# Linear attention and a two-layer network in one kernel: keys and values with the token halves on the partition halves

## The chip, the cores and the metric

The kernel runs on one core of one Trainium2 chip. The metric is device time in microseconds (us); shorter is better. The kernel before takes 294.94 us, the median of 8 runs (294.67 to 295.29).

A core's engines, as the profile names them: PE (TensorE, matmuls; PEld is its weight load), DVE (VectorE), ACT (ScalarE), POOL (GpSimd, which here issues the loads) and SP (SyncE, which issues stores and small transfers).

## The reference

```python
def _attn_ref(q, k, v):                      # each [8 batches, 8 heads, 576 tokens, 64]
    phi = lambda x: np.where(x > 0, x, np.exp(x) - 1.0) + 1.0
    q_p, k_p = phi(q), phi(k)
    kv = np.einsum('bhsd,bhse->bhde', k_p, v)
    z = np.sum(k_p, axis=2)
    num = np.einsum('bhsd,bhde->bhse', q_p, kv)
    den = np.einsum('bhsd,bhd->bhs', q_p, z)[..., None] + 1e-06
    return num / den

def _moe_ref(x, w_in, w_out):                # x: [4608, 512], the heads side by side
    h = x @ w_in                             # w_in [512, 2048]
    return (h - np.tanh(h)) @ w_out          # w_out [2048, 512]
```

Inputs and output are float32; the kernel computes matmuls in bfloat16 with float32 sums.

## The kernel before, in words

**The dense part.** The 4608 tokens are taken in nine chunks `c` of 512. For a chunk, the first layer (`l1mm`, L366) computes 16 blocks `fi` of 128 hidden rows, each as four matmuls (one for each pair of heads `p`) into one PSUM bank of 512 float32 columns; ACT takes tanh and DVE the difference (`l1act`, `l1act2`), which gives `gT`. The second layer (`l2mm`, L387) runs in 16 slots `s` of four matmuls. In chunk 0 the slots go by groups of `w_out` first: slots 0 to 3 use group 0, 4 to 7 group 1, 8 to 11 group 2 and 12 to 15 group 3. `evac` (L396) copies the output by ACT, and SP stores it.

**Attention between it.** The work of attention is hung by hand on these steps. `s1[fi]` lists what is done behind block `fi` of the first layer, `s2[s]` what is done behind slot `s` of the second. For chunk `c` that is the attention of batch `c + 1` (products and division) and the loads and phi of batch `c + 2`. Every engine works off its own list strictly in this written order. Two chunks aren't regular: in chunk 0 batch 1 is computed in the second layer (slots 7 to 15), with TensorE transposes (`a_qT_pe`, L164) and the reciprocal spread by matmuls (`spread1`: `a_spread_pe`, L354, and `a_scale`, L359); before chunk 0 stands the opening, which makes batch 0 in small steps (`b0_...`) while matmuls on zeros (`spin`, L444) fill PE's time.

**One batch.** `load_k`, `load_q` and `load_v` are DMAs that POOL issues, with a cast to bfloat16 on the way. A tile is `[128, 2 (h), 2 (i), 9 (j), 64]`: a partition half holds one head of a pair, each partition nine tokens `j`, and `(h, i)` names the pair. One tensor is one DMA of 512 rows of 1152 bytes (two DMAs for batch 0, L90). `phi_pieces` computes phi as min(exp x, max(x, 0) + 1): `e` on ACT, `r` and the minimum on DVE (L134 to L136). The key/value product (`a_kv_cols`, L199, for batches 2 to 7; `a_kv`, L177, for batch 1) has for each `i` nine tokens `j`, and for each `j` two matmuls of 64 rows, one on each partition half, with 136 or 192 columns: 36 matmuls. A masked multiply on DVE (L186, L202) gives `kz`: the key/value blocks and, in 32 columns, the sums z of the keys. `a_vp` (L189) lays the values out for it. `a_den` (L276) multiplies z with q's transposes; the reciprocal (L285) and, for batch 1, `a_split` follow on DVE. For batches 2 to 7 `a_spread` sends the reciprocals through DRAM to all partitions (`ds`, `rdb`, on SP's queue), and `a_num` (L317, L328) multiplies. For batch 1, `num1` computes num into four banks (L317, L320), which ACT copies to `ns` (L344, L346).

**Queues.** All loads go through POOL in program order: q and k of batch 0, then v, ten pieces of `w_in` (L110), k of batch 1, two groups of `w_out` (L115), q and v of batch 1, two groups of `w_out`; from slot 4 of chunk 0 on q, k and v of batch 2; later batches behind `gate` (L383), which waits for the transposed q of the batch before. That transpose is a DMA on SP's queue (`a_qT_dma`, L153).

Of the kernel before, what the change touches and what calls it, by code (L numbers as in the profile page):

```python
# [18 lines left out]
def kernel(  # L19
# [17 lines left out]
    J = S // 64  # L37

# [56 lines left out]

    def load_k(b):
        k_t[b] = kpool.tile([128, 2, 2, J, D], BF16, name="kraw")
        load(b, k_t[b], k, b == 0)
# [5 lines left out]
    def load_v(b):  # L104
        load(b, v_b[b % 2][:, 0:2], v, b == 0)
# [15 lines left out]
    def phi_pieces(b, src, store, name, i, parts=0):  # L121
# [4 lines left out]
        e = epool.tile([128, 2, J, D], BF16, name="e")  # L126
        r = epool.tile([128, 2, J, D], BF16, name="r")
        y = store[b][:, i].rearrange("p j h d -> p h j d")
        if parts:

            return ([lambda h=h: nc.scalar.activation(e[:, h], x[:, h], AF.Exp) for h in range(2)],
                    lambda: nc.vector.tensor_scalar(r, x, 0.0, 1.0, ALU.max, ALU.add),
                    [lambda h=h: nc.vector.tensor_tensor(y[:, h], e[:, h], r[:, h], ALU.min) for h in range(2)])
# [38 lines left out]
    def kv_mm(b, i, ps):  # L172
        kp, vt = kp_t[b], v_b[b % 2]
        for j in range(J):
            for hg in range(2):
                r = slice(64 * hg, 64 * hg + 64)
                nc.tensor.matmul(ps[hg], kp[r, i, j].rearrange("p h d -> p (h d)"),  # L177
                                 vt[r, :, i, j, :], start=(j == 0), stop=(j == J - 1))

    def a_kv(b, banks):  # L180
        kz_t[b] = kz_c[b % 2]
        ps = [banks()[:, 0:384].rearrange("p (i e) -> p i e", i=2) for hg in range(2)]
        for i in range(2):
            kv_mm(b, i, [ps[hg][:, i, :] for hg in range(2)])
# [6 lines left out]
    def a_kv_cols(b, banks):  # L191
        kp = kp_t[b]
        kz_t[b] = kz_c[b % 2]
        ps = [banks()[:, 0:272].rearrange("p (i e) -> p i e", i=2) for hg in range(2)]
        for i in range(2):
            for j in range(J):
                for hg in range(2):
                    r = slice(64 * hg, 64 * hg + 64)
                    nc.tensor.matmul(ps[hg][:, i, :], kp[r, i, j].rearrange("p h d -> p (h d)"),  # L199
                                     vp[r, i, j, :], start=(j == 0), stop=(j == J - 1))  # L200
# [4 lines left out]
    def b0_z(i):  # L205

        for j in range(J):
            for hg in range(2):
                r = slice(64 * hg, 64 * hg + 64)
                nc.tensor.matmul(ps_all[:, 4 - 2 * i + hg, 0:32], kp_t[0][r, i, j].rearrange("p h d -> p (h d)"),  # L210
                                 one[r, 0:32], start=(j == 0), stop=(j == J - 1))

    def b0_zc(i):
        nc.vector.tensor_mul(kz_t[0][:, :, i, 128:160], ps_all[:, 4 - 2 * i:6 - 2 * i, 0:32], mask[:, :, i, 128:160])

    def b0_kv(i):

        for j in range(J):
            for hg in range(2):
                r = slice(64 * hg, 64 * hg + 64)  # L220
                nc.tensor.matmul(ps_all[:, 2 * i + hg, 0:128], kp_t[0][r, i, j].rearrange("p h d -> p (h d)"),
                                 v_b[0][r, 0:2, i, j, :], start=(j == 0), stop=(j == J - 1))

    def b0_kz(i):
        nc.vector.tensor_mul(kz_t[0][:, :, i, 0:128], ps_all[:, 2 * i:2 * i + 2, 0:128], mask[:, :, i, 0:128])

    def b0_num(i, ns):

        kz, qT, b0 = kz_t[0], qT_t[0], 2 * i
        for hg in range(2):  # L230
            nc.tensor.matmul(ps_all[:, b0 + hg, :].rearrange("p (j t) -> p j t", j=8), kz[:, hg, i, 0:128],
                             qT[:, i, 0:8, hg, :], start=True, stop=True)
        nc.scalar.copy(ns[:, i::2, 0:8, :].rearrange("p a j t -> p a (j t)"), ps_all[:, b0:b0 + 2, :])
# [231 lines left out]
    for f in mk1:  # L465
        f()
# [176 lines left out]
```

## Time and profile before

| what | value |
|---|---|
| median of 8 runs | 294.94 us |
| the profiled execution: its time, its span | 294.84 us, 293.1 us |
| granted TensorE clock, mean | 0.998 |
| first dense matmul (L366); dense matmuls without a break from | 16.48 us; 17.74 us |
| second layer of chunk 0; its slot 8; first layer of chunk 1 | 31.14; 41.15; 51.08 us |
| L366, L387: 128x512 matmuls | 576 and 560, 128.0 and 127.8 us busy |
| L199, 64x136 matmuls (batches 2 to 7) | 216, 7.4 us busy |
| loads through POOL (software queue) | 17552 packets, 18.35 MB, 38.8% of the engines' time |

How to read it: a row of the profile names the line, the engine and the operation, with what it writes and reads, the shapes, the number of instructions, and the busy time and mean time of one. "Idle before, releaser" is the time in which the engine stood still just before, and what ended that. A timeline row has the start in us, the busy time of the row's instructions together, and their number. Consecutive matmuls overlap in their pipeline: a matmul's own time (379 ns for 512 columns) is longer than the distance to the next one (216 ns), so costs are read from start to start.

### The profile page before, as it was taken

Reading aid. Unit: us, or ns where it says so; the run is one execution under the profiler, and the core shown is the slowest. Engines: PE = TensorE matmul, PEld = TensorE weight load, DVE = VectorE, ACT = ScalarE, POOL = GpSimd, SP = SyncE. Lnnn points to the kernel's source line nnn. Section 1 sums busy time; section 2 is a strip of 40 time slices with the busy share of each in tenths; the row PEclk is TensorE's granted clock in tenths of the full one; section 3 lists DMA queues with packets and bytes.
Section 4 is the critical chain, followed back from the end, with each engine's and each line's share of the span. In section 5 each row is a group of like instructions: output and inputs, shape, how many; then the busy total and the mean of one; then the engine's idle time right before and its main releaser. Section 6 shows DMA issues by size and latency. Waiting matters only on the chain.

```text
span 293.1 us, 4504 instructions
## 1 busy us (share of the span) xinstructions
PE 285.2 (97%) x1801; PEld 134.2 (46%) x1801; DVE 174.5 (60%) x265; ACT 139.5 (48%) x168; POOL 33.5 (11%) x55
## 2 busy tenths in 40 slices
PE   8899999999999999999999999999999999999994
PEld 2544453454444444444444444444444444444443
DVE  4759857887567764786478646865581456106600
ACT  3938537947344643455246524661452155126411
POOL 8573030030030003000300020000000000000000
PEclk9999999999999999999999999999999999999999
DMA  6999999997999658954895669577107310131032
GB/s 99 196 204 213 207 207 217 205 144 141 240 162 190 160 117 139 218 138 108 135 223 129 138 134 182 103 186 144 38 20 181 73 36 0 38 82 25 0 74 72
DMA packets 39077, 38.94 MB, mean 133 GB/s; under 512 B 16336, under 2 KB 33808, under 8 KB 38288
## 3 DMA queue, kind: packets, MB, share of 16 engines
q0 software_dynamic: 17552, 18.35, 38.8%
q1 hardware_dynamic: 21344, 20.17, 30.1%
q8 instruction: 14, 0.23, 0.3%
q10 hardware_dynamic: 160, 0.13, 0.1%
q14 instruction: 7, 0.06, 0.1%
HBM read 43.91 MB, written 9.55 MB: 182 GB/s over the span
## 4 chain that ended last, share of the span: by engine, by line
PE 73%; DMA 15%; issue 7%; POOL 2%; DVE 1%; SPq 0%; ACT 0%; POOLq 0%; DVEq 0%
PE ps_all L366 35%; PE ps_all L387 32%; DMA qraw<-in_q_dram 6%; DMA w_in_sb<-in_moe_w_in_dram 3%; DMA rdb<-ds 3%; PE ps_all L199 2%; DMA kraw<-in_k_dram 2%; PE ps_all L317 2%; DMA ds<-rden 1%; PE ps_all L604 1%; PE ps_all L276 1%; POOL qraw L90 0%; ACT e L134 0%; DVE rden L285 0%; SPq L305 0%
## 5 line engine op out<-in xcount | busy, mean ns | idle before, releaser
L366 PE MATMUL ps_all<-xT,w_in_sb 128*128 128x512 bf16 x576 | 128.0, 379 | 0.3 <-DVE xT L244 0.3
L387 PE MATMUL ps_all<-w_out_sb,gT 128*128 128x512 bf16 x560 | 127.8, 379 | 0.0
L373 DVE TENSOR_TENSOR gT<-ps_all,th 128x1024 bf16<-128x1024 f32 x64 | 77.9, 1218 | 59.8 <-ACT th L372 59.8
L372 ACT ACTIVATE th<-ps_all 128x1024 f32<-128x1024 f32 x64 | 65.5, 1024 | 57.0 <-PE ps_all L366 47.1
L366 PEld LDWEIGHTS <-w_in_sb 128*128 128x128 bf16 x576 | 55.2, 98 | 66.7 <-issue 0.6
L387 PEld LDWEIGHTS <-gT 128*128 128x128 bf16 x560 | 54.0, 98 | 64.5 <-issue 0.5
L396 ACT COPY osb<-ps_all 128x512 f32<-128x512 f32 (+1 forms) x36 | 20.9, 583 | 73.6 <-PE ps_all L387 54.4
L328 DVE TENSOR_TENSOR xT<-ps_all,rdb 128x512 bf16<-128x512 f32 x24 | 16.3, 689 | 13.6 <-PE ps_all L317 11.2
L134 ACT ACTIVATE e<-qraw 128x1152 bf16<-128x1152 bf16 x16 | 18.5, 1161 | 6.8 <-DMA qraw<-in_q_dram 6.8
L134 ACT ACTIVATE e<-kraw 128x1152 bf16<-128x1152 bf16 x15 | 17.5, 1165 | 0.3 <-DMA kraw<-in_k_dram 0.3
L136 DVE TENSOR_TENSOR qp<-e,r 128x1152 bf16<-128x1152 bf16 x16 | 12.0, 757 | 7.8 <-ACT e L134 7.2
L136 DVE TENSOR_TENSOR kp<-e,r 128x1152 bf16<-128x1152 bf16 x15 | 11.4, 758 | 8.4 <-ACT e L134 7.5
L383 POOL COPY g<-qT 1x1 bf16<-1x1 bf16 x5 | 1.1, 225 | 120.8 <-DMA qT<-qp 120.8
L378 DVE TENSOR_TENSOR gT<-ps_all,th 128x512 bf16<-128x512 f32 x16 | 10.3, 684 | 2.4 <-ACT th L377 1.7
L377 ACT ACTIVATE th<-ps_all 128x512 f32<-128x512 f32 x16 | 9.2, 599 | 4.3 <-PE ps_all L366 3.1
L317 PE MATMUL ps_all<-qT,kz 128*128 128x512 bf16 x28 | 10.1, 379 | 0.1
L444 PE MATMUL ps_all<-zero 128*128 128x512 bf16 x29 | 8.6, 455 | 1.2 <-DVE zero L405 1.2
L135 DVE TENSOR_SCALAR r<-qraw 128x1152 bf16<-128x1152 bf16 x16 | 7.2, 453 | 2.2 <-DMA qraw<-in_q_dram 2.2
L199 PE MATMUL ps_all<-vp,kp 64*128 64x136 bf16 x216 | 7.4, 220 | 0.4 <-POOL g L383 0.4
L199 PEld LDWEIGHTS <-kp 64*128 64x128 bf16 x216 | 6.4, 94 | 3.0 <-issue 2.1
L285 DVE RECIPROCAL rden<-den 128x144 f32<-128x144 f32 x7 | 7.4, 1053 | 0.2
L394 DVE COPY osb<-ps_all 128x128 f32<-128x128 f32 x1 | 0.3, 292 | 11.6 <-PE ps_all L604 11.6
(82 smaller groups left out, 121.8 us busy)
## 6 DMA issues: line engine op xcount, KB each, us to landing
out_dram<-osb SPq DMA_DIRECT2D x70, 128.0 KB
rdb<-ds SPq DMA_DIRECT2D x12, 576.0 KB
kraw<-in_k_dram POOLq DMA_DIRECT2D x7, 576.0 KB, 6.9
qraw<-in_q_dram POOLq DMA_DIRECT2D x7, 576.0 KB, 9.1
v<-in_v_dram POOLq DMA_DIRECT2D x7, 576.0 KB, 11.9
w_out_sb<-in_moe_w_out_dram POOLq DMA_DIRECT2D x4, 512.0 KB, 16.0
w_in_sb<-in_moe_w_in_dram POOLq DMA_DIRECT2D x6, 256.0 KB, 8.6
qraw<-in_q_dram POOLq DMA_DIRECT2D x2, 288.0 KB, 4.7
```

The lines of the kernel that those rows point to most:

```text
L134: return (lambda: nc.scalar.activation(e, x, AF.Exp), lambda: nc.vector.tensor_scalar(r, x, 0.0, 1.0, ALU.max, ALU.add), lambda: nc.vector ...
L136: lambda: nc.vector.tensor_tensor(y, e, r, ALU.min))
L199: nc.tensor.matmul(ps[hg][:, i, :], kp[r, i, j].rearrange("p h d -> p (h d)"), vp[r, i, j, :], start=(j == 0), stop=(j == J - 1))
L317: nc.tensor.matmul(ps, kz[:, p // 2, p % 2, 0:128], qT[:, p % 2, 0:8, p // 2, :], start=True, stop=True)
L328: nc.vector.tensor_mul(xT[:, p, S * b:S * b + 512].rearrange("p (j t c) -> p j t c", j=8, t=4), ps.rearrange("p j (t c) -> p j t c", t=4), ...
L366: nc.tensor.matmul(h, w_in_sb[:, 2 * (p % 2) + p // 2, fi * 128:(fi + 1) * 128], xT[:, p, c * 512:(c + 1) * 512], start=(n == 0), stop=(n ...
L372: nc.scalar.activation(th, h, AF.Tanh)
L373: nc.vector.tensor_sub(gT[:, fi:fi + 2, :], h, th)
L377: nc.scalar.activation(th, h, AF.Tanh)
L378: nc.vector.tensor_sub(gT[:, fi, :], h, th)
L387: nc.tensor.matmul(o, gT[:, fi, i * 128:(i + 1) * 128], w_out_sb[:, fi, :], start=(fi == 0), stop=(fi == NF - 1))
L396: nc.scalar.copy(osb[:, f0:f1], o[:, f0:f1])
```

## The change

1. `load_kv` takes the place of `load` for k and v, for all batches. Heads go in pairs with a member `g`. The tokens of head `g = 0` stand on both partition halves in slots 0 to 3 and, for one half, in slot 4; head `g = 1` has the other half of slot 4 and slots 5 to 8. Four DMAs write a tensor, each to 64 partitions, with rows of 640 or 512 bytes.
2. Every product over the tokens goes through `over_tokens`: for each `i` four matmuls of 128 rows (slots 0 to 3), one of 64 rows on the lower half, one of 64 rows on the upper half (slot 4), and four of 128 rows (slots 5 to 8). That is 20 matmuls for 36, with the same columns.
3. The opening follows these slots. `phi_slots` computes phi of batch 0's keys in the cuts that the loads have: three exps, two `r`, four minima. The sums z are started with slots 0 to 3 of both `i` and copied by one multiply (`b0_zc`) instead of two; `b0_kv`, `b0_kz` and `b0_num` go by the member `g` instead of `i`; `a_den` of batch 0 stands behind `b0_kv(0)` and `b0_kz(0)`. The pairs of chunk 0's first blocks go 0, 1, 2, 3 instead of 0, 2, 1, 3.
4. In chunk 0 batch 1's product stands between its two sets of transposes: the second set moves from slot 7 to slot 8. den, num and the split stand together in slot 9 (before: den in 9, num and split in 10).
5. phi of batch 2's queries, with the DMA transpose, is in slots 13, 14 and 15 instead of 12, 13 and 14, and batch 2's product in chunk 1 behind block 8 instead of 7.

```diff
+    def load_kv(b, t, src):
+        x = src[b].rearrange("(n g) (p j) d -> g p n (j d)", g=2, j=J)
+        for g, half, s0, s1, j0 in ((0, 0, 0, 5, 0), (0, 1, 0, 4, 5), (1, 1, 4, 9, 0), (1, 0, 5, 9, 5)):
+            nc.gpsimd.dma_start(
+                out=t[64 * half:64 * half + 64, :, :, s0:s1].rearrange("q h i j d -> q (h i) (j d)"),
+                in_=x[g, :, :, D * j0:D * (j0 + s1 - s0)])
...
-        load(b, k_t[b], k, b == 0)
+        load_kv(b, k_t[b], k)
...
-        load(b, v_b[b % 2][:, 0:2], v, b == 0)
+        load_kv(b, v_b[b % 2][:, 0:2], v)
...
+    ALL, LO, HI = slice(0, 128), slice(0, 64), slice(64, 128)
+    steps = [(ALL, j, 0) for j in range(4)] + [(LO, 4, 0), (HI, 4, 1)] + [(ALL, j, 1) for j in range(5, J)]
+    def over_tokens(b, i, rhs, out, which=range(10)):
+        for n in which:
+            r, j, g = steps[n]
+            nc.tensor.matmul(out[g], kp_t[b][r, i, j].rearrange("p h d -> p (h d)"), rhs(r, j),
+                             start=n in (0, 5), stop=n in (4, 9))
...
+    def phi_slots():
+        kp_t[0] = work.tile([128, 2, J, 2, D], BF16, name="kp")
+        y = kp_t[0].rearrange("p i j h d -> p h i j d")
+        x = k_t[0]
...
+        return ([lambda: nc.scalar.activation(e[0], x[:, :, :, 0:4], AF.Exp)]
+                + [lambda i=i: nc.scalar.activation(e[1][:, :, i], x[:, :, i, 4:J], AF.Exp) for i in range(2)],
...
     def a_kv_cols(b, banks):
...
         for i in range(2):
-            for j in range(J):
-                for hg in range(2):
-                    r = slice(64 * hg, 64 * hg + 64)
-                    nc.tensor.matmul(ps[hg][:, i, :], kp[r, i, j].rearrange("p h d -> p (h d)"),
-                                     vp[r, i, j, :], start=(j == 0), stop=(j == J - 1))
+            over_tokens(b, i, lambda r, j: vp[r, i, j, :], [ps[hg][:, i, :] for hg in range(2)])
...
+    def b0_kv(g):
+        for i in range(2):
+            o = ps_all[:, 7 - 4 * g, 128 * i:128 * i + 128]
+            over_tokens(0, i, lambda r, j: v_b[0][r, 0:2, i, j, :], [o, o], range(5 * g, 5 * g + 5))
...
-    for f in (ek0, rk0, *ek1, mk0, rk1):
+    for f in (ek[0], rk[0], ek[1], ek[2], mk[0], mk[1], rk[1]):
...
-    b0_z(0)
-    for f in mk1:
-        f()
-    b0_zc(0)
+    for i in range(2):
+        b0_z(i, range(4))
+    for i in range(2):
+        mk[2 + i]()
+        b0_z(i, range(4, 10))
+    b0_zc()
     b0_kv(0)
     b0_kz(0)
-    b0_z(1)
-    b0_zc(1)
-    a_den(0, Banks([4]))
+    a_den(0, Banks([6]))
...
-            s2[7].append(lambda: (a_qT_pe(1, 0, side), a_qT_pe(1, 1, side), a_kv(1, side)))
-            s2[8].append(lambda: b0_scale_rest(side))
-            s2[9].append(lambda: a_den(1, side))
-            s2[10].append(lambda: (num1(), a_split(1)))
+            s2[7].append(lambda: (a_qT_pe(1, 0, side), a_kv(1, side)))
+            s2[8].append(lambda: (a_qT_pe(1, 1, side), b0_scale_rest(side)))
+            s2[9].append(lambda: (a_den(1, side), num1(), a_split(1)))
...
-            s2[12].append(lambda: q2(0))
-            s2[13].append(lambda: (spread1(1), q2(1)))
-            s2[14].append(lambda: q2(2))
-            s2[15].append(lambda: a_kphi(2, 0))
+            s2[13].append(lambda: (spread1(1), q2(0)))
+            s2[14].append(lambda: q2(1))
+            s2[15].append(lambda: (q2(2), a_kphi(2, 0)))
         elif n1 < B:
-            s1[7 if c == 1 else 5].append(lambda: a_kv_cols(n1, attn))
+            s1[8 if c == 1 else 5].append(lambda: a_kv_cols(n1, attn))
```

## The prediction on record

> **What bounds the kernel now.** I read the page first, then the chain of waits, then the timeline of single engines in the stretches that the change touches.
>
> ```profile
> PE 285.2 (97%) x1801; PEld 134.2 (46%) x1801; DVE 174.5 (60%) x265; ACT 139.5 (48%) x168; POOL 33.5 (11%) x55
> ...
> DMA  6999999997999658954895669577107310131032
> GB/s 99 196 204 213 207 207 217 205 144 141 240 162 190 160 117 139 218 138 108 135 223 129 138 134 182 103 186 144 38 20 181 73 36 0 38 82 25 0 74 72
> ```
>
> The span is 293.1 us and PE is busy in 97% of it. But in the first nine slices of 7.3 us (to about 60 us) the DMA engines are full as well. So there are two stages: before 42 us PE and the loads run a race, afterwards only PE's own work and its few gaps count. Here is the race, from PE's timeline and, below it, the issues of the second pair of w_out loads in POOL's timeline and the landing of the first of that pair:
>
> ```profile
> 40.56 0.66 PE L177 MATMUL ps_all<-v,kp 64*128 64x192 bf16 x12
> 41.15 1.04 PE L387 MATMUL ps_all<-w_out_sb,gT 128*128 128x512 bf16 x4
> ...
> 45.32 1.03 PE L387 MATMUL ps_all<-w_out_sb,gT 128*128 128x512 bf16 x4
> 47.04 0.31 PE L354 MATMUL ps_all<-w,sel 32*128 32x144 bf16 x8 [0.69 <-ACT ns L344]
> 47.28 1.90 PE L387 MATMUL ps_all<-w_out_sb,gT 128*128 128x512 bf16 x8
> ```
>
> ```profile
> 23.17 1.50 POOL L115 DMA_DIRECT2D w_out_sb<-in_moe_w_out_dram  x2
> ```
>
> ```profile
> DMA to landing us min/median/max: 17.9/17.9/17.9
> ```
>
> The second layer's slot 8 (41.15) is the first to use w_out group 2. That load is issued at 23.17 and lands 17.9 us later, at 41.1: PE finds it with no slack. Also to be seen: a gap of 0.85 us before L354 (four matmuls from 45.32 at 0.216 us end at 46.19; PE goes on at 47.04, when ACT's copies of num free the banks).
>
> In the steady part the key/value product stands between the first layer's matmuls like this (c = 2):
>
> ```profile
> 86.40 1.03 PE L366 MATMUL ps_all<-xT,w_in_sb 128*128 128x512 bf16 x4
> 87.36 1.24 PE L199 MATMUL ps_all<-vp,kp 64*128 64x136 bf16 x36
> 88.53 0.60 PE L366 MATMUL ps_all<-xT,w_in_sb 128*128 128x512 bf16 x2
> ```
>
> The last L366 ahead starts at 87.05, the next one at 88.53: 1.48 us, of which 0.216 are that L366. So the product costs 1.27 us. The two of a pair (64 rows each) start 4 ns apart, and pairs follow at 58.7 ns, about the time of one full-row matmul of 136 columns. Thus 18 pairs make 1.05 us. The rest, 0.2 us, is at the two ends: L199 starts 0.31 us after L366 where L366 after L366 takes 0.216, and L366 starts 0.15 us after the last pair instead of 0.06. Each change between 128 rows and 64 rows costs 0.095 us. It isn't the wait for a semaphore: L317 behind L387, both 128 rows, starts after 0.22.
>
> **1. Products of batches 2 to 7 (20 matmuls for 36).** Each i has four full-row matmuls, two of 64 rows (a pair), four full-row ones. Full-row matmuls of 128 columns, each with its own weights, follow at 55.6 ns (L164, nine in 0.50), so 136 columns take 59. Streaming: 16 x 59 + 2 x 59 = 1.06 us, as before; the halves ran side by side, so filling the rows saves nothing. But the rows change four times (into and out of each pair) instead of twice: 4 x 0.095 + 1.06 = 1.44 against 1.27, **+0.18 us per batch**. No row shows a change inside one accumulation; bounds are 0 per change (-0.20 per batch) and twice the measured one (+0.55). I take 0.095, which the ends of L199, L177 and the col-tiled L276 all show. Nothing hides it: PE is the bound there. Batches 3 to 7: +0.9 us.
>
> [...] The trace has 55.6 for L164. [...]
>
> **2. Loads of k and v: four DMAs of 64 partitions for one of 128 (two for batch 0).** Rows of 1152 bytes become 640 and 512. POOL needs 0.62 us per issue (w_in's median, 64 partitions) instead of 0.75, so 2.5 us per tensor for 0.75 (1.5 for batch 0); POOL is 11% busy. The page's waits show POOL waiting at w_in's fifth issue for k, and so on: eight are in flight. After the change w_in's first issue waits for k's first piece (about 8.5 us instead of 6.33), but its landing is set by the queue ahead: the DMA engines never pause. So the price is transfer time. In 12 to 16 us, with mostly 512-byte packets, the queue moved 195 GB/s in 1341 packets; in 42 to 50, with mostly 1152-byte ones, 209 GB/s. w_in's first 128 KB pieces land 0.66 us apart, a whole tensor takes 2.85. Both give +0.1 to +0.2 us per tensor split in four; I take 0.12. Below 0 isn't to be had, since the bytes are the same. The upper bound is 0.6: single packets take 107 ns at 1152 bytes, 60 at 512 and by interpolation 70 at 640, if they didn't overlap. Ahead of w_out group 2 stand k and v of batches 0 and 1: 4 x 0.12 = 0.5, so it lands at 41.6.
>
> [...]
>
> **3. The opening.** q is as before. k's first two pieces (slots 0 to 3) land at about 9.2, where the first half landed (9.16). Then exp of 1024 (1.05), two minima of 512 and, after the last piece (10.7), two exps of 640 (0.73 each, from 576 at 0.68) to 12.05, a last minimum to 12.6, z's second half with two changes of rows, one masked multiply (about 0.29, between 0.215 for 64 and 0.424 for 256) to 13.4. Before, z was copied at 13.28 and half of den had been done. Now kv(0) and its multiply stand before den: den ends about 14.6 and the reciprocal about 15.7 instead of 14.75. I take the dense stream 0.9 us later (17.74 to 18.6); bounds 0 (equal waits) and 2.
>
> What lies behind: PE's slots 0 to 7 end at 38.0 + 0.9. Then one transpose set (0.51) and batch 1's product, now in the middle, without the 0.4 us wait for qp that stood between the sets; 18 pairs of 192 columns took 1.59, with four row changes about 1.87. PE reaches slot 8 at 41.3; the load allows it at 41.65. **So the opening and the reordered transposes are paid by the wait for w_out**; slot 8 starts 0.5 us later. If the opening is 2 us later, 0.8 of it comes through.
>
> **4. Slot 8 to the end of c = 0.** Before: 9.93 us (41.15 to 51.08). Added: the second transpose set, 0.51. Removed: nearly all of the 0.85 us gap and 0.1 at den's entry, since two slots (1.73 us) now lie between num and the spread; ACT's five copies took 2.65 us from num's start and end in time. What is late next is DVE's reciprocal chain: 3.23 us from den's start to w, about 0.2 us beyond PE; so the gap shrinks to about 0.1 to 0.2. Now 9.77: -0.16. Sum so far: c = 1 starts 0.34 us later.
>
> **5. Batch 2 one slot later.** Its exps now come after osb 1 and 2, so ACT's first tanh pair of c = 1 starts 2.76 us after c = 1 begins instead of 2.36; DVE's chain behind it (gT, k's minimum, gT, vp) is 0.4 later too. Before, PE waited 0.53 us for vp at L199 (58.52). Now the product stands one slot on and finds vp done, but slot 8 of the first layer waits for its bank (gT of pair 2/3, at about 7.4 us) for 0.5 us: the gap moves, it doesn't go. With +0.18 for the product: **+0.2 us**. On SP the transposing DMA of qT is issued 1.4 us later, with it POOL's loads of batch 3, which meet the rdb transfer (71.0 to 78.9); L317 already waited 0.22 us for it at 79.81. I take +0.1, bounds 0 and 1.4.
>
> **Sum:** 0.5 - 0.16 + 0.2 + 0.1 + 0.9 = +1.5 us. The profiled execution took 294.84 us (span 293.1, 1.7 around it): 296.4. The runs' median is 294.94, so +0.1 at most; I forecast **296.4**.
>
> **Rivals.**
> - *Faster: changes of rows inside the product cost nothing.* For it: the accumulation has no wait between. Against: L276 to L231 at 13.57 changes without a wait too, and costs 0.1. Then -0.2 per batch: 0.5 - 0.16 - 0.18 + 0 - 1.0 = -0.84, 294.0. The sign turns where a change costs about 0.04 us, with the terms of the opening as above. 0.22.
> - *Cancelled:* split packets cost nothing, slot 8 stays at 41.2, and batch 2's wait goes: -0.1 - 0.35 + 0.9 = +0.4, 295.2. For it: no byte more. 0.18.
> - *Longer:* packets cost as single ones do (4 x 0.6 = 2.4 in place of 0.5: 298.3), or the opening is 2 us late (+0.8: 297.2), or rdb is caught by the late loads (+1.3: 297.7). 0.12, all near or above 297.2.
> - Forecast, 295.6 to 297.2: 0.48.
>
> A difference below 0.2% (0.6 us, 294.35 to 295.5) can't be told from none here. Faster: 0.20 (of the first rival). Same: 0.18 + 0.02. Slower: 0.48 + 0.12. The range 293.9 to 297.6 leaves out the far ends of the first and the third rival.
>
> **What the new profile would show.** Right: the product of c = 2 from L366 to L366 takes 1.66 us (not 1.48), with gaps of about 0.15 around its two pairs; w_out group 2 lands near 41.6 and PE waits for it; the gap before the spread is below 0.3; the first L366 stands near 17.3. Wrong: a product of 1.3 us; a landing beyond 43; PE late at slot 8 with the load long there.

## The result, and the profile after

The changed kernel takes 298.80 us (median of 11 runs, 296.93 to 300.89), the kernel before 294.91 us beside it (31 runs, 294.42 to 295.78): a ratio of 1.0136, 95% interval 1.0117 to 1.0155. So it is 1.4% slower. The direction is the forecast one, the size isn't: 296.4 was forecast, and 298.80 lies outside 293.9 to 297.6. The spread of the runs has also grown, from 1.4 to 4.0 us; that is part of what has to be explained.

The profiled execution took 300.89 us, its span is 299.1 (before 293.1): 6.0 us more. Three lines of the page after (busy time, granted clock in 40 slices, DMA share):

```profile
PE 290.2 (97%) x1657; PEld 136.8 (46%) x1657; DVE 174.8 (58%) x265; ACT 139.4 (47%) x168; POOL 59.2 (20%) x101
...
PEclk9959999999999999999999999999999999999999
DMA  7999999769999687967898779787108310131032
```

PE has 144 matmuls fewer (1657 for 1801) and yet is 5.0 us longer busy. The third digit of the clock, a 5, is the new thing: before, the granted clock was 1.00 from 4.96 to 291.7 us. POOL's 25.7 us more are its issues.

Where the 6.0 us come from, in milestones of PE (us from the span's start). The last column is a second profile of the same changed kernel (the run a9_again below, 301.07 us):

| | before | after | after again |
|---|---|---|---|
| first matmul of the first layer | 16.48 | 19.03 | 17.84 |
| second layer, slot 0 | 31.14 | 34.87 | 32.49 |
| slot 8 | 41.15 | 44.19 | 42.34 |
| c = 1 | 51.08 | 53.95 | 52.10 |
| c = 2 | 82.08 | 87.00 | 86.85 |
| c = 3 | 112.44 | 117.56 | 117.72 |
| span | 293.1 | 299.1 | 299.3 |

Two profiles with the same sum, but the loss sits at different places: 2.9 us before c = 1 and 2.0 in it, or 1.0 and 3.7. Each later chunk costs 0.21 us more in both (30.565 for 30.354; 30.87 the first time in the second profile).

**The opening.** PE's timeline after, and then the busy time and clock by stretches (columns: window, us, PE, PEld, DVE, ACT, POOL, granted clock, DMA share, GB/s) of after and of before:

```profile
15.40 1.59 PE L125 MATMUL ps_all<-v,kp 64*128 64x128 bf16 x10
16.91 1.24 PE L257 MATMUL ps_all<-rden,sel 32*128 32x128 f32 x16
```

```profile
12.00:15.00 3.00, 2.52 (x44) 1.58 (x44) 1.55 (x4) 2.32 (x7) 2.58 (x5) 1.00 1.43 188
15.00:22.00 7.00, 7.00 (x51) 3.53 (x50) 3.01 (x6) 2.02 (x2) 3.90 (x7) 0.51 1.26 202
```

```profile
12.00:15.00 3.00, 2.76 (x80) 1.85 (x80) 2.36 (x7) 2.93 (x8) 1.81 (x3) 1.00 1.37 192
15.00:22.00 7.00, 6.66 (x56) 3.25 (x57) 3.86 (x7) 2.59 (x5) 5.32 (x8) 1.00 1.26 205
```

From 15.03 to 21.85 us PE was granted half its clock. The 16 spreading matmuls of L257 took 1.24 us for 0.73 before (L240). A busy share of 100% hides it: PE is "busier" because it is slower. It stands still in no part of this stretch (7.00 of 7.00 us busy), so it waits for no other engine.

**The product of c = 2:**

```profile
90.88 1.46 PE L383 MATMUL ps_all<-xT,w_in_sb 128*128 128x512 bf16 x6
92.18 1.65 PE L125 MATMUL ps_all<-vp,kp 128*128 128x136 bf16 x20
93.67 0.59 PE L383 MATMUL ps_all<-xT,w_in_sb 128*128 128x512 bf16 x2
```

The sixth L383 starts at 90.88 + 5 x 0.216 = 91.96, the next at 93.67: 1.71 us (1.48 before, 1.66 forecast). Inside, full-row matmuls follow at 59 ns; from the last of them to the pair are 0.155 us, from the pair to the next 0.161, so a change of rows costs about 0.1.

**The wait in c = 1.** PE's timeline after, at the first num that needs the second transfer of rdb, and the two transfers in the chain of waits after:

```profile
81.92 1.03 PE L404 MATMUL ps_all<-w_out_sb,gT 128*128 128x512 bf16 x4
84.72 0.38 PE L334 MATMUL ps_all<-qT,kz 128*128 128x512 bf16 x1 [1.78 <-DVE xT L345]
```

```profile
69.52 5.04 DMA ds<-rden
75.21 8.65 DMA rdb<-ds
```

The last L404 starts at 82.57 and leaves the way free at 82.78, so PE waits 1.94 us (0.21 before). The transfers took 5.04 and 8.65 us; before they took 4.16 and 7.90. Below, "the rdb wait" is always this gap, worked out so. SP's timeline after and before shows one reason why they meet more traffic:

```profile
51.83 6.72 SPq L418 DMA_DIRECT2D out_dram<-osb  x8
58.67 2.89 SPq L186 DMA_TRANSPOSE qT<-qp  x1
68.42 1.39 SPq L322 DMA_DIRECT2D ds<-rden  x4
```

```profile
48.96 4.18 SPq L401 DMA_DIRECT2D out_dram<-osb  x6
53.26 2.61 SPq L153 DMA_TRANSPOSE qT<-qp  x1
65.24 1.29 SPq L305 DMA_DIRECT2D ds<-rden  x4
```

The transposing DMA of batch 2 stood behind six stores and now stands behind all eight: it is issued 4.7 us after the start of c = 1 instead of 2.2. POOL's loads of batch 3 wait for it (first issue 64.12 for 58.65), and they take 14.6 us from first issue to last landing instead of 11.6, so the last lands at 78.8, 3.5 us after the rdb transfer has begun (75.21). Before, it had landed at 70.2, ahead of it (71.04).

### The profile page after: what moved, and what is told of

It reads as the page before. It is cut to its first block, busy times and chain, and to the rows that moved or that the text cites. A ratio compares the mean times of both kernels' runs of the same rounds, so it can differ in the third digit from the quotient of the medians.

```text
span 299.1 us, 4305 instructions
## 1 busy us (share of the span) xinstructions
PE 290.2 (97%) x1657; PEld 136.8 (46%) x1657; DVE 174.8 (58%) x265; ACT 139.4 (47%) x168; POOL 59.2 (20%) x101
## 3 DMA queue, kind: packets, MB, share of 16 engines
q0 software_dynamic: 26480, 18.36, 42.3%
## 4 chain that ended last, share of the span: by engine, by line
PE 82%; DMA 9%; ACT 3%; DVE 2%; issue 1%; POOL 1%; SPq 1%; DVEq 0%; ACTq 0%; POOLq 0%
PE ps_all L383 39%; PE ps_all L404 34%; PE ps_all L125 4%; DMA rdb<-ds 3%; DMA out_dram<-osb 2%; DMA kraw<-in_k_dram 2%; PE ps_all L334 2%; DMA ds<-rden 2%; ACT osb L413 1%; PE ps_all L293 1%; DVE gT L390 1%; PE ps_all L257 1%; ACT e L167 1%; POOL kraw L102 1%; PE ps_all L248 1%
## 5 line engine op out<-in xcount | busy, mean ns | idle before, releaser
L383 PE MATMUL ps_all<-xT,w_in_sb 128*128 128x512 bf16 x576 | 128.9, 381 | 0.4 <-DVE gT L390 0.4
L404 PE MATMUL ps_all<-w_out_sb,gT 128*128 128x512 bf16 x560 | 127.7, 379 | 0.0
L383 PEld LDWEIGHTS <-w_in_sb 128*128 128x128 bf16 x576 | 55.6, 98 | 66.8 <-issue 2.0
L404 PEld LDWEIGHTS <-gT 128*128 128x128 bf16 x560 | 54.2, 98 | 66.1 <-issue 2.1
L102 POOL DMA_DIRECT2D kraw<-in_k_dram x32 | 19.7, 633 | 5.6 <-issue 3.2
L102 POOL DMA_DIRECT2D v<-in_v_dram x32 | 20.0, 669 | 3.6 <-DMA qraw<-in_q_dram 3.6
L167 ACT ACTIVATE e<-kraw 128x1152 bf16<-128x1152 bf16 x14 | 16.3, 1165 | 0.0
L169 DVE TENSOR_TENSOR kp<-e,r 128x1152 bf16<-128x1152 bf16 x14 | 10.6, 757 | 7.5 <-ACT e L167 6.7
L125 PEld LDWEIGHTS <-kp 128*128 128x128 bf16 (+1 forms) x180 | 11.1, 98 | 6.6 <-issue 1.3
L125 PE MATMUL ps_all<-vp,kp 128*128 128x136 bf16 (+1 forms) x120 | 9.9, 225 | 0.0
```

The source lines that it names most:

```text
L102: nc.gpsimd.dma_start(out=t[64 * half:64 * half + 64, :, :, s0:s1].rearrange("q h i j d -> q (h i) (j d)"), in_=x[g, :, :, D * j0:D * (j0 ...
L125: nc.tensor.matmul(out[g], kp_t[b][r, i, j].rearrange("p h d -> p (h d)"), rhs(r, j), start=n in (0, 5), stop=n in (4, 9))
L167: return (lambda: nc.scalar.activation(e, x, AF.Exp), lambda: nc.vector.tensor_scalar(r, x, 0.0, 1.0, ALU.max, ALU.add), lambda: nc.vector ...
L169: lambda: nc.vector.tensor_tensor(y, e, r, ALU.min))
L383: nc.tensor.matmul(h, w_in_sb[:, 2 * (p % 2) + p // 2, fi * 128:(fi + 1) * 128], xT[:, p, c * 512:(c + 1) * 512], start=(n == 0), stop=(n ...
L404: nc.tensor.matmul(o, gT[:, fi, i * 128:(i + 1) * 128], w_out_sb[:, fi, :], start=(fi == 0), stop=(fi == NF - 1))
```

## The experiments

The theory, A in the texts below: the forecast's sum stands, and two things come on top that it left out or made too small: the half clock in the opening and the rdb wait. The rivals of these texts: B, the cut loads are what costs, through w_out; C and E, the cut loads alone make the rdb wait; D, the 20 matmuls are slow for another reason than the changes of rows; F, the clock halves by chance. Two more have no letter: the new opening is slow of itself, with or without the clock; and the late transposing DMA alone makes the rdb wait.

### The opening: is it the clock?

**a1_spin**, after with six more matmuls on zeros in the opening (they compute nothing that is used), so that PE works more before 15 us:

```diff
     for i in range(2):
         b0_z(i, range(4))
+    spin(2)
     for i in range(2):
         mk[2 + i]()
         b0_z(i, range(4, 10))
+        spin(1)
...
     a_den(0, Banks([6]))
+    spin(2)
```

> The changed kernel with six more matmuls on zeros (2 behind the first part of z, 1 behind each second part, 2 behind den), nothing else. Theory A (the opening lost PE's clock: the trace after shows half the clock from 15.03 to 21.85 us, because PE was too little busy just before): the granted clock stays at 1.0 through the opening, the dense stream starts near 19 us instead of 21.15, the runs no longer spread over 4 us, and the time falls from 298.8 to about 297. Theory B (the loss is the loads, cut in four): the clock may recover, but the median stays within 0.5 us of 298.8, since PE then waits for w_out in slot 8.

Measured: 297.88 us (297.36 to 301.2), ratio 1.0124 (1.0068 to 1.0180). Stretches of a1_spin:

```profile
12.00:15.00 3.00, 3.00 (x46) 1.65 (x46) 1.56 (x4) 2.08 (x7) 2.37 (x4) 1.00 1.41 181
15.00:22.00 7.00, 6.65 (x62) 3.40 (x61) 3.41 (x6) 2.39 (x3) 3.88 (x7) 1.00 1.27 204
...
84.00:87.50 3.50, 3.50 (x14) 1.42 (x13) 2.17 (x5) 0.59 (x1) 1.57 (x3) 0.58 0.69 154
```

The opening keeps its clock: first L383 at 17.79 instead of 19.03, slot 8 at 41.86 instead of 44.19. But in this run PE waited 2.92 us for rdb, and right behind that wait the clock was halved for 3.41 us (84.57 to 87.98). So the half clock has two places, and the second one was on neither theory's list; by this one run the spread stays at 3.8 us, against the expectation (the other three lie within 0.7 us).

**a7_less_spin**, the other way: after without the last six zero matmuls ahead of z.

```diff
-    spin(6)
```

> The changed kernel without the six matmuls on zeros that stand ahead of z (the last group of them, from 9.98 us on), nothing else; PE waits there for k's minimum anyway. Theory A (PE's clock halves where PE is too little busy in the stretch before 15 us): half the clock after the opening in most or all runs (before: some of the runs), mean clock at or below 0.990, and a median of 300 or more. Rival F (the clock halves by chance, whatever PE does there): as many runs with the clock at 0.998 or more as in the changed kernel.

Measured: 301.70 us (299.38 to 303.56), ratio 1.0234 (1.0174 to 1.0294). Stretches of a7_less_spin:

```profile
12.00:15.00 3.00, 2.46 (x43) 1.60 (x44) 1.55 (x5) 2.38 (x8) 2.50 (x5) 0.95 1.43 191
15.00:22.00 7.00, 7.00 (x51) 3.44 (x50) 2.74 (x5) 2.02 (x2) 3.82 (x7) 0.53 1.26 198
```

Taking work away makes it slower. Half clock from 14.69 to 21.5; all four runs have a mean clock of 0.981 to 0.987. In the runs that have after's opening unchanged (after, a3_q2early, a4_pairs, a9_again: 26 runs) six show 0.986 to 0.989, which is what 6.83 us at half rate make of 299 (3.4 / 299 = 0.011). The mean doesn't tell the place; the profiles of after and a3_q2early do. With six zero matmuls more (a1_spin, a5_three, a6_spin_q2early) it is none of 14 (two have 0.994, and their profiles show the halving at the later place). None of 14, six of 26, four of four: the chance of a half clock goes with the work of PE in that stretch. (None of 14 beside six of 26 could still be luck, about one time in 17; four of four hardly, one in 130.)

What differs from run to run can be read from the traces. The changes of the clock in after, at 4.79, 15.03, 21.85 and 298.33 us, lie 3, 2 and 81 steps of 3.413 us apart, and the two in before, at 4.96 and 291.68 us, 84 steps. The half clock of a3_q2early (14.81 to 21.64) lasts two steps, as in after; behind the rdb wait it lasts one, in a1_spin as in a9_again and a5_three. Against the kernel this grid isn't fixed: a point of it is at 15.03 us in after, at 14.81 in a3_q2early, at 15.20 in before (three steps behind 4.96) and at 15.78 in a9_again (20 steps ahead of the half clock at 84.05). The thin stretch meets it differently: in after most of it falls into one window of the grid (11.61 to 15.03), and the clock halves at that window's end; in a9_again, the same kernel, it is shared by two windows, and the clock stays. a5_three (below) has nearly the grid of after, but six zero matmuls more, and keeps its clock. These windows of after, a9_again (two) and a5_three:

```profile
11.61:15.03 3.42, 2.57 (x45) 1.58 (x44) 1.92 (x5) 2.71 (x8) 3.00 (x5) 1.00 1.42 189
8.95:12.37 3.42, 2.67 (x30) 1.55 (x29) 2.65 (x7) 2.81 (x4) 2.56 (x5) 1.00 1.36 185
12.37:15.78 3.41, 2.98 (x48) 1.68 (x44) 1.86 (x4) 2.37 (x8) 2.85 (x6) 1.00 1.42 187
11.66:15.08 3.42, 3.22 (x48) 1.83 (x48) 1.95 (x5) 2.62 (x8) 2.93 (x5) 1.00 1.38 185
```

PE's busy time alone doesn't tell the windows apart: behind 2.57 us busy the clock halved, behind 1.99 us (after, 83.29 to 86.71) it didn't. A matmul's own time, which busy time adds up, hardly depended on its rows: with 136 columns, one of 64 rows took 230 ns in the mean and one of 128 rows 224 (L125 in after). Weighted by rows and columns from the shapes, at 216 ns for a 128x512 matmul on 128 columns of weights, the first of these two windows holds about 1.1 us and the second about 1.9. In the half clock itself the two windows (15.03 to 18.44, 18.44 to 21.85) hold 1.0 and 1.3, and behind the second the clock is back at 1.00. In before the last window ahead of the half clock at 291.68 us holds about 0.9, every other one from 4.96 us on at least about 1.9. This is an estimate from the shapes and starts of the matmuls in after and before, made afterwards; no run tests it.

**a2_oldopen**, after, but batch 0 loaded and computed as before (loads uncut, 64-row products, old order):

```diff
-        load_kv(b, k_t[b], k)
+        load(b, k_t[b], k, True) if b == 0 else load_kv(b, k_t[b], k)
...
+        for j in range(J):
+            for hg in range(2):
+                r = slice(64 * hg, 64 * hg + 64)
```

> The changed kernel, but batch 0 as in the kernel before: its loads in halves, its phi, its sums, its order of pairs. Batches 1 to 7 and all slots stay as changed. Theory A: the dense stream starts at 17.7 us as before, the clock stays at 1.0, slot 8 starts at 41.3 to 41.7 (w_out group 2 lands there), and the time is about 297; what is left above 294.9 is the four changes of rows per batch (1.3) and the wait for rdb (up to 1.7). Theory B (the loads of batches 1 on, cut in four): still above 298.

Measured: 297.07 us (296.83 to 297.24), ratio 1.0072 (1.0057 to 1.0087). No half clock, and the spread is gone. This is nearly the forecast's own sum (its profiled run took 297.04, forecast 296.4; over it are some 0.3 us of rdb wait and 0.2 of products), because the forecast held the opening to be hidden. The rdb wait is only 0.64 us here, with the late transposing DMA and the cut loads both in place. PE's timeline of a2_oldopen at slot 8:

```profile
41.69 1.02 PE L395 MATMUL ps_all<-w_out_sb,gT 128*128 128x512 bf16 x4 [0.88 <-DMA w_out_sb<-in_moe_w_out_dram]
```

Slot 8 waits for w_out group 2 and starts at 41.69 (forecast 41.65). The new opening is also slow of itself, in part: with the clock held, it uses up this 0.88 us of cover and 0.2 to 0.3 us more (slot 8 at 41.86 in a1_spin, 42.02 in a6_spin_q2early, without a wait for w_out).

### The rdb wait: late transposing DMA, or cut loads?

**a3_q2early**, after with batch 2's q back in its old slots:

```diff
-            s2[13].append(lambda: (spread1(1), q2(0)))
-            s2[14].append(lambda: q2(1))
-            s2[15].append(lambda: (q2(2), a_kphi(2, 0)))
+            s2[12].append(lambda: q2(0))
+            s2[13].append(lambda: (spread1(1), q2(1)))
+            s2[14].append(lambda: q2(2))
+            s2[15].append(lambda: a_kphi(2, 0))
```

> The changed kernel with phi of batch 2's queries and its transposing DMA back in slots 12, 13 and 14 (the product of batch 2 stays behind block 8). Theory A (the transpose is queued on SP behind the stores of the last output block, so the loads of batch 3 start 2.5 us later against PE than before and collide with the rdb transfer): the transpose is issued about 2 us earlier against the start of chunk 1, the wait of L334 for rdb shrinks from 1.95 us to 0.2 to 0.8, the time falls by 1.2 to 1.7 us against the changed kernel (at the same clock). Rival C (the rdb transfer is late because of the cut loads alone): the wait stays at 1.5 us or more.

Measured: 297.05 us (296.22 to 299.64), ratio 1.0084 (1.0050 to 1.0117). The rdb wait falls to 0.69 us (from 1.94), with the same half clock in the profiled opening (14.81 to 21.64). That fits the late transposing DMA as one cause, but one pair of profiles doesn't show it: the wait differs as much between profiles that all have q late (see the end of "Back together").

**b3_q2late**, the reverse, before with the late slots (and batch 2's product behind block 8), and **b1_split**, before with k and v of batches 1 to 7 in four DMAs of 64 partitions:

```diff
-            s2[12].append(lambda: q2(0))
-            s2[13].append(lambda: (spread1(1), q2(1)))
-            s2[14].append(lambda: q2(2))
-            s2[15].append(lambda: a_kphi(2, 0))
+            s2[13].append(lambda: (spread1(1), q2(0)))
+            s2[14].append(lambda: q2(1))
+            s2[15].append(lambda: (q2(2), a_kphi(2, 0)))
...
-            s1[7 if c == 1 else 5].append(lambda: a_kv_cols(n1, attn))
+            s1[8 if c == 1 else 5].append(lambda: a_kv_cols(n1, attn))
```

> The kernel before, with phi of batch 2's queries and its transposing DMA in slots 13, 14 and 15 and batch 2's product behind block 8, nothing else. Theory A: the transpose stands on SP behind all eight stores of chunk 0, is issued 2 us or more later (55.5 instead of 53.26), the loads of batch 3 follow, and the wait of L317 for rdb grows from 0.22 to 0.8 to 1.5 us; the time rises by 0.8 to 1.5 us. Rival C: no wait above 0.4 us, the time within 0.4 us.

```diff
+        for half, s0, s1 in ((0, 0, 5), (1, 5, 9), (1, 0, 5), (0, 5, 9)):
+            nc.gpsimd.dma_start(
+                out=t[64 * half:64 * half + 64, :, :, s0:s1].rearrange("q h i j d -> q (h i) (j d)"),
+                in_=x[64 * half:64 * half + 64, :, D * s0:D * s1])
```

> The kernel before, with k and v of batches 1 to 7 loaded by four DMAs of 64 partitions each (rows of 640 and 512 bytes, the old places of the tokens), nothing else. Theory A (late loads against rdb and the rows' changes make the loss): w_out group 2 lands 0.2 to 0.3 us later, slot 8 starts at 41.4, chunk 2 starts 0.3 to 0.7 us later than 82.08, the time rises by 0.3 to 0.7 us. Rival C (the cut loads alone delay rdb): L317 waits for rdb 1.5 us or more, the time rises by 1.5 to 3 us.

Measured: b3_q2late 295.28 us, ratio 1.0009 (1.0000 to 1.0018); b1_split 295.73 us, ratio 1.0026 (1.0015 to 1.0038). Their rdb waits, first b1_split, then b3_q2late:

```profile
81.20 0.38 PE L325 MATMUL ps_all<-qT,kz 128*128 128x512 bf16 x1 [1.05 <-DVE xT L336]
```

```profile
80.10 0.38 PE L317 MATMUL ps_all<-qT,kz 128*128 128x512 bf16 x1 [0.45 <-DVE xT L328]
```

By the gap that is 1.21 and 0.61 us (before 0.21). The cut loads alone lengthen the wait; for the late transpose that is hardly told, since b2_slots, which has neither, waits 0.45 us. Neither reaches 1.94. Both results lie between theory and rival and miss both: b1_split with +0.79 us, b3_q2late with +0.34. In b3_q2late the transposing DMA is issued only 0.9 us later against c = 1 (3.0 us behind its start instead of 2.2), not 2 us or more as in after, so a delay as long as that one was not tested alone. In b1_split the loads of batch 3 take 13.5 us instead of 11.6.

**b5_rows** and **b6_halves** take the cut apart: before with two DMAs of 128 partitions and short rows (640 and 512 bytes), or with two of 64 partitions and whole rows.

```diff
+        for s0, s1 in ((0, 5), (5, 9)):
+            nc.gpsimd.dma_start(out=t[:, :, :, s0:s1].rearrange("q h i j d -> q (h i) (j d)"),
+                                in_=x[:, :, D * s0:D * s1])
```

> The kernel before, with k and v of batches 1 to 7 loaded by two DMAs of 128 partitions each, cut within the rows (640 and 512 bytes), nothing else. If the short rows make the loss of the run with the cut loads (+0.8 us, k, q and v of batch 3 land in 13.5 us instead of 11.6, L317 waits 1.2 us for rdb): the same here, about 295.7 and 13 us or more. If the partition halves or the number of DMAs make it: about 295.0 and 12 us.

```diff
+        for half in range(2):
+            nc.gpsimd.dma_start(out=t[64 * half:64 * half + 64].rearrange("q h i j d -> q (h i) (j d)"),
+                                in_=x[64 * half:64 * half + 64])
```

> The kernel before, with k and v of batches 1 to 7 loaded by two DMAs of 64 partitions each, with whole rows of 1152 bytes, nothing else. If the partition halves make the loss of the run with the cut loads: about 295.7, and k, q and v of batch 3 land in 13 us or more. If the short rows make it: about 295.0 and 11.6 to 12 us.

Measured: 295.53 us, ratio 1.0021 (1.0011 to 1.0031), and 295.36 us, ratio 1.0024 (1.0012 to 1.0037); rdb waits 0.69 and 0.41 us, loads of batch 3 in 12.4 and 13.2 us. Two pieces cost nearly what four do, whichever way the cut runs. Neither row length nor the number of partitions is singled out; the mechanism stays open.

### The changes of rows

**a4_pairs**, after with both `i` in one run, so that the four 64-row matmuls stand together: two changes of rows per product instead of four.

```diff
+        for i, n in ([(0, n) for n in range(4)] + [(1, n) for n in range(6, 10)] + [(0, 4), (1, 5), (1, 4), (0, 5)]
+                     + [(1, n) for n in range(4)] + [(0, n) for n in range(6, 10)]):
...
-        for i in range(2):
-            over_tokens(b, i, lambda r, j: vp[r, i, j, :], [ps[hg][:, i, :] for hg in range(2)])
+        over_both(b, lambda i, r, j: vp[r, i, j, :], ps)
```

> The changed kernel with the two 64-row pairs of a product of batches 1 to 7 next to each other (slots 0 to 3 of i=0, 5 to 8 of i=1, the four 64-row matmuls, the rest), so that the rows change twice per product and not four times. Theory A: a product from the last L383 ahead to the next one takes 1.52 us instead of 1.71 (two changes of 0.095 less), a chunk 30.37 us instead of 30.565, and the time falls by about 1.1 us at the same clock. Rival D (the 20 matmuls cost the 0.2 us for another reason, such as longer weight loads of 128 rows): no change.

Measured: 296.76 us (295.53 to 297.41), ratio 1.0066 (1.0044 to 1.0088). The product of c = 2 in a4_pairs:

```profile
87.23 0.81 PE L391 MATMUL ps_all<-xT,w_in_sb 128*128 128x512 bf16 x3
87.88 1.44 PE L135 MATMUL ps_all<-vp,kp 128*128 128x136 bf16 x20
89.15 0.81 PE L391 MATMUL ps_all<-xT,w_in_sb 128*128 128x512 bf16 x3
```

From 87.66 (the third L391) to 89.15 are 1.49 us (before 1.48), and the chunk takes 30.36 us (30.354 before, 30.565 after). So the 0.21 us per chunk are the two additional changes, and 20 matmuls cost no less than 36: the filled rows save nothing. D is out. The time fell by 2.0 us, more than the 1.1 expected; that is not the products alone, since the runs differ in the wait and the clock too (the profiled one kept its clock in the opening and waited 0.40 us for rdb, with q late).

### Back together

**a6_spin_q2early** is a1_spin with a3_q2early's edit, **a5_three** has a4_pairs' edit as well, **a8_old_pairs_q2early** is a2_oldopen with the edits of a3_q2early and a4_pairs.

> The changed kernel with the six more matmuls on zeros in the opening and batch 2's queries back in slots 12 to 14. Theory A (two losses that vary from run to run: half the clock after the opening, and the wait for rdb): no run has half the clock in the opening; the wait for rdb is below 1 us; the runs lie within 0.8 us of each other, at about 296.3. Rival E (the wait for rdb comes from the cut loads, wherever the queries stand): the wait stays at 1 us or more in the profile, and the runs spread over 1.5 us or more.

Measured: 297.17 us (297.05 to 297.28), ratio 1.0084 (1.0069 to 1.0099). With the clock held in both places (every run at 0.998 or more) the spread is 0.2 us. It is 0.9 above what was expected: slot 8 stands at 42.02 (0.9 later than before, the forecast had 0.5) and the rdb wait is 0.90 us (before 0.21).

> As the one before it, and with the two pairs of each product next to each other (two changes of rows for four). Theory A: another 1.1 us less, about 295.2; what is left above the kernel before is then the cut loads (0.8 in the run with the cut loads alone) less the gain of the slots (0.4). Rival D: the same time as the one before it.

Measured: 296.51 us (295.77 to 299.0), ratio 1.0074 (1.0040 to 1.0107), 1.3 above what was expected. In the profiled run (299.0) the rdb wait was 2.26 us although q is early, and behind it the clock halved (83.34 to 86.75). So early q doesn't always cure the wait: a miss.

> Batch 0 as in the kernel before; batches 1 to 7 with the changed places of the tokens and cut loads, but with the pairs next to each other and batch 2's queries in slots 12 to 14. What is left of the change is the cut loads, the slots 7 to 9 and the product behind block 8. By the sum of the runs with one part alone: 294.9 + 0.8 (cut loads) - 0.4 (slots and block 8) = 295.3, slot 8 at 41.6, a chunk 30.36 us. Rival: 294.5 or less, if full rows save something that the changes of rows have covered so far.

Measured: 295.43 us (295.06 to 296.01), ratio 1.0026 (1.0013 to 1.0039). With old opening, joined pairs and early q, 0.7 us of the 3.9 are left, as expected (295.3), and the rival is out; the rdb wait is 0.55 us and c = 1 starts at 51.47.

**a9_again** is after itself, unchanged.

> The changed kernel once more, for more runs and another profile. Theory A: runs with the mean clock at 0.999 or more lie between 296.9 and 298.8 and differ by the wait for rdb; a run with the clock at 0.990 or less lies above 299. In the profile, time minus 294.9 is the sum of 1.3 (products), 0.5 (slot 8 behind w_out, if the clock held in the opening, else about 3), and the wait for rdb.

Measured: 299.10 us (296.65 to 301.07), ratio 1.0116 (1.0055 to 1.0177). Its profile: the opening at full clock with the same PE work as in after (first fence), and the wait in c = 1 (second):

```profile
12.00:15.00 3.00, 2.51 (x44) 1.59 (x44) 1.55 (x5) 2.33 (x7) 2.51 (x5) 1.00 1.41 187
15.00:22.00 7.00, 6.65 (x62) 3.39 (x61) 3.66 (x6) 2.34 (x3) 4.38 (x7) 1.00 1.27 202
```

```profile
83.20 0.38 PE L334 MATMUL ps_all<-qT,kz 128*128 128x512 bf16 x1 [2.11 <-DVE xT L345]
83.42 1.27 PE L404 MATMUL ps_all<-w_out_sb,gT 128*128 128x512 bf16 x4
84.91 1.91 PE L404 MATMUL ps_all<-w_out_sb,gT 128*128 128x512 bf16 x4
```

After a wait of 2.27 us four L404, 1.03 us in after, take 1.27 and then 1.91: half clock from 84.05 to 87.46. So one kernel takes either loss, or neither (296.65). The expected sum is a miss: 1.3 + 0.5 + 2.3 us make 4.1, and 6.2 were measured. It left out the half clock behind the wait (1.7 us), and slot 8 stands 1.2 us later instead of 0.5.

Put together, the rdb waits don't sort by the place of q. With q late and the loads cut they are 0.40 (a4_pairs), 0.64 (a2_oldopen), 1.67 (a7_less_spin), 1.94 (after), 2.27 (a9_again) and 2.92 us (a1_spin); with q early and the loads cut 0.55 (a8_old_pairs_q2early), 0.69 (a3_q2early), 0.90 (a6_spin_q2early) and 2.26 (a5_three). By the times early q does gain something: a6_spin_q2early ends below every run of a1_spin, by some 0.5 us at the median of those at full clock; of this, 0.38 us is den of batch 2, which comes 11.24 us after the start of c = 1 instead of 11.62. The chain of waits shows where a long wait arises, and it is not always the same place. In after both transfers are slower (5.04 and 8.65 us for 4.16 and 7.90). In a9_again and a1_spin one of SP's four issues of `ds` took 1.71 and 1.25 us, and `ds` then 4.87 and 5.67. In a5_three `ds` took 5.88. That issue in after (first fence), and in a9_again with the transfer behind it:

```profile
68.76 0.37 SPq L322
```

```profile
66.91 1.71 SPq L322
68.67 0.42 SPq L322
69.13 4.87 DMA ds<-rden
```

### The part that gains

**b2_slots**, before with part 4 of the change (num beside den, one transpose set behind slot 7, one behind slot 8), and **b4_slots_kv8**, the same with batch 2's product behind block 8 and its q in the old slots:

```diff
-            s2[7].append(lambda: (a_qT_pe(1, 0, side), a_qT_pe(1, 1, side), a_kv(1, side)))
-            s2[8].append(lambda: b0_scale_rest(side))
-            s2[9].append(lambda: a_den(1, side))
-            s2[10].append(lambda: (num1(), a_split(1)))
+            s2[7].append(lambda: (a_qT_pe(1, 0, side), a_kv(1, side)))
+            s2[8].append(lambda: (a_qT_pe(1, 1, side), b0_scale_rest(side)))
+            s2[9].append(lambda: (a_den(1, side), num1(), a_split(1)))
```

> The kernel before, with batch 1's product between its sets of transposes and den, num and split together in slot 9, nothing else. By my sum, slot 8 starts at 41.15 as before, since w_out group 2 lands there, although PE is ready about 1 us earlier; slots 8 to 15 take 9.77 us instead of 9.93, and the time falls by 0.1 to 0.3 us. Rival: the wait for w_out isn't there, slot 8 starts near 40.2, and the time falls by 1 us.

Measured: 294.96 us, ratio 1.0001 (0.9992 to 1.0010): no gain that can be told.

```diff
-            s1[7 if c == 1 else 5].append(lambda: a_kv_cols(n1, attn))
+            s1[8 if c == 1 else 5].append(lambda: a_kv_cols(n1, attn))
```

> As the kernel before it, and batch 2's product in chunk 1 behind block 8 instead of 7, with phi of batch 2 in its old slots. By my sum the wait of 0.53 us for vp at the product goes and slot 8's bank comes free in time, so the time falls by 0.4 to 0.6 us more: about 294.1 to 294.4, below both kernels. Rival: the wait moves on (to den behind block 10, or to rdb), and the time stays within 0.2 us of the kernel before it.

Measured: 294.50 us (294.28 to 295.00, 10 runs), ratio 0.9984 (0.9975 to 0.9994). It beats both kernels, by little. PE's timeline of b4_slots_kv8:

```profile
41.20 1.02 PE L387 MATMUL ps_all<-w_out_sb,gT 128*128 128x512 bf16 x3 [0.86 <-DMA w_out_sb<-in_moe_w_out_dram]
...
44.99 1.89 PE L387 MATMUL ps_all<-w_out_sb,gT 128*128 128x512 bf16 x7
46.92 0.30 PE L354 MATMUL ps_all<-w,sel 32*128 32x144 bf16 x8
```

PE reaches slot 8 0.86 us early and the load holds it there, so the earlier transposes are hidden; behind it c = 1 starts at 50.96 (51.08). From there to den of batch 2 it takes 11.03 us instead of 11.30: batch 2's product no longer waits for its values.

## Why the prediction was wrong

**Step 1 (products) was right.** 1.71 us for 1.66, 0.21 us per chunk for 0.18. The first rival, that changes of rows cost nothing, is refuted by a4_pairs.

**Step 2 (cut loads) was right where it was worked out, in the opening.** Group 2 of w_out lands at 41.7 in a2_oldopen (41.6 forecast; 42.3 in a9_again, the latest). (Its upper bound was added up too low: at the 107, 70 and 60 ns that it names, 512 rows on 16 engines cost 0.7 us more, not 0.6; nothing hangs on it.) The step left out batch 3's loads: there the four-way cut costs 1.9 us of landing (b1_split), with 1.0 us more of waiting for rdb in that profile.

**Step 3 (the opening) failed.** "I take the dense stream 0.9 us later (17.74 to 18.6); bounds 0 (equal waits) and 2". The delay was worked out from waits alone, at full clock. With full clock the stream starts 1.3 to 1.4 us later (19.05 in a1_spin, 19.10 in a9_again), inside the bounds; part of this is a wait that was overlooked: kv(0) writes bank 7, from which ACT copies qT until 13.04, so it starts at 13.09 (0.05 us behind that copy; the same in a9_again, a1_spin, a3_q2early and a7_less_spin). Batch 1's product took 2.01 us (39.85 to 41.86 in a1_spin) for 1.87. In other runs the clock halves at about 15 us for 6.83 us, and the stream starts at 21.15 (after), 3.4 later and beyond the upper bound; 3.0 us of this reach slot 8. The step counted matmuls removed only as time saved. That PE's work in this stretch holds the clock is shown by taking zero matmuls out (a7_less_spin, a mean clock of 0.981 to 0.987 in all four runs) and putting them in (a5_three, 1.00 behind 11.66 to 15.08); that the loss in after comes from the matmuls which the change removed is inferred from that.

**Step 4 was right, in part by luck.** 9.76 us from slot 8 to c = 1 (9.77 forecast), 0.2 us of gap ahead of the spread. But the terms as written add up to 9.6 or 9.7, and one of them, the 0.1 us at den's entry, did not go (46.53 to 46.63 in after).

**Step 5 (batch 2 one slot later) failed in its second term.** The place of the product came out at +0.32 us for +0.2 (den of batch 2, counted from c = 1). "The gap moves, it doesn't go" holds only as long as q is late: with q early it goes (b4_slots_kv8, -0.27). But of the transposing DMA it said "L317 already waited 0.22 us for it at 79.81. I take +0.1, bounds 0 and 1.4". The wait grew by 1.7 us in the profiled run, by 2.1 and 2.7 in a9_again and a1_spin, and by as little as 0.2 in a4_pairs: the term was made too small, and its upper bound too. The DMA was taken to be 1.4 us later; with two more stores ahead of it on SP's queue it is 2.5 later against c = 1 in after, but 0.9 in a2_oldopen and 1.8 in a1_spin. Its effect was priced without the cut loads of batch 3, which land 1.9 us later on their own, with 1.0 us more of wait (b1_split). What makes up the rest is located in the chain of `ds` and rdb, not explained. Where a wait of 2.26 to 2.92 us fell wholly or mostly into one window of the clock's grid, the clock halved once again (a1_spin, a5_three, a9_again), which is another 1.7 us; the 1.94 us of after lie across an edge of the grid (83.29), the 1.67 of a7_less_spin left PE 1.90 us busy in their window, and the clock stayed.

The rival "longer" (0.12) had a late opening and a late rdb, but one at a time, at 297.2 and 297.7, and not the clock. A wait of 1.9 to 2.9 us alone leads beyond the end of the range at 297.6.

So with the clock held and q early the kernel takes a6_spin_q2early's 297.17; by difference the other 1.6 us to the median of 298.80 are left for the longer wait and the half clocks, in shares that vary from run to run. Seven of the 11 runs have a mean clock of 0.997 or more and still take 296.93 to 299.54; the profiles that there are point to the wait, but there is none of these seven.

**What stays open:** why batch 3's loads take 0.8 to 1.9 us longer in two or four pieces when the opening's hardly do; how much of the rdb wait is the late transposing DMA's; why SP's issue of `ds` and the two transfers are slower in some runs than in others; and whether the weighted work in a window is what the clock goes by.

## What to carry to other kernels

Before taking matmuls out of a stretch in which PE waits in small pieces, look at the granted clock there: here the clock went with work that PE seemed to do for nothing (a7_less_spin: six matmuls on zeros fewer, and a mean clock of 0.981 to 0.987 in all four runs). When a step is moved, count what stands ahead of it on every queue it issues to, and bound the wait behind it with all delays that may meet there, instead of each by itself. One profile of a kernel whose runs spread over 4 us isn't enough to name a cause: look at the same wait in every profile. Filling the rows saved nothing here, where the half-row matmuls already ran side by side (the two of a pair start 4 ns apart), and each change between the two forms cost about 0.1 us.

## What the runs showed of the hardware

- The clock was granted at 1.00 or 0.50 in before and after, and its changes lay whole steps of 3.413 us apart (84 in before; 3, 2 and 81 in after). It halved for 3.41 us behind rdb waits of 2.26, 2.27 and 2.92 us (a5_three, a9_again, a1_spin), and for 6.83 us in the openings of after and a3_q2early. In after PE was busy for 2.57 of the 3.42 us ahead of that, with no wait longer than 0.38 us.
- A full-row bfloat16 matmul of 136 columns with its own weights followed the one before at 59 ns, and a change between 128 and 64 rows cost about 0.1 us inside a product (0.155 and 0.161 us where full rows follow at 0.059, in after) as well as at its ends (0.31 us from start to start where it is 0.216 without a change, and 0.15 for 0.06, in before).
